# Splitting the first load of a decode kernel by partitions: 16 rows of wq first, then the other 112

## The chip, the cores and the metric

The kernel runs on one core of a Trainium2 chip. The metric is the device time of one execution in microseconds (us). Executions of this kernel fall into a fast and a slow state: the kernel before takes about 193.2 us in the one and about 196.5 us in the other, so only fast runs are compared with fast runs.

## The reference, cut to what matters

```python
g = sigmoid((x * gate_w).sum(-1))            # x: [1, 1, 512]
q = x @ wq                                   # wq: [512, 4096] bf16, 4 MB: 32 heads of 128
p = softmax(q @ k.T * 128 ** -0.5)           # k, v: [32 heads, 4096 keys, 128] bf16, 32 MB each
a = (p @ v) @ wo                             # wo: [4096, 512], 4 MB
b = relu(x @ w1 + b1) ** 2 @ w2 + b2         # w1: [512, 1376], w2: [1376, 512]
return g * a + (1 - g) * b
```

One token passes over 78.3 MB of weights and cache. Each byte is used once.

## The kernel before

The parts that the change and the argument touch, cut ("..." marks what is left out). SBUF is the memory on the core that the loads write; the large buffers of this kernel have 128 partitions. All large loads are issued by one engine (SP), so they stand in one queue (q1 of the page: 78.32 of the 78.41 MB), in the order of the code:

```python
wq_t = A_wq.rearrange("(p t) n -> p (t n)", t=4)     # 128 rows of 32 KB, contiguous in memory
wbig = sb("wbig", [128, 16384], bf16)                # one row for each SBUF partition
...
d_wq = P.dma("sp", "wq", lambda e: e.dma_start(wbig[:, :], wq_t))
...                       # q = x @ wq: 32 matmuls on TensorE; the first waits for all of d_wq
def load_k(p):            # 8 loads of [128, 16384] (32 KB a partition), two buffers
    d_k.append(P.dma("sp", f"k{p % 2}", lambda e: e.dma_start(
        Kt[:, p % 2, :], k_t[p]), prods.get((p - 2, NC - 1))))
def load_v(p):
    d_v.append(P.dma("sp", f"v{p % 2}", lambda e: e.dma_start(
        Vt[:, p % 2, :], v_t[p]), pvs.get(p - 2)))
...                       # order in the queue: wq, k0, k1, v0, k2, v1, ... k7, v6, v7
d_w1 = ...                # then w1, wo in three parts,
d_w2r = P.dma("sp", "w2r", lambda e: e.dma_start(w2_r, B_w2[128 * NJ:F, :]), k_free)
...                       # (the line above: the last 96 rows of w2, on 96 partitions) and w2 in three parts
```

The softmax here doesn't subtract the row's maximum and nothing guards it: scores larger than these inputs give would overflow.

## Time and profile before

| | the kernel before |
|---|---|
| time | 193.6 us median of 3 runs (192.99 to 193.73); 193.66 median of the 4 runs beside the change, one of them slow (196.65) |
| span of the profile shown first (slow state) | 194.5 us |
| span of a second profile, fast state, taken later as a control | 191.3 us |
| bytes loaded | 78.3 MB, 403 GB/s over the 194.5 us |

The page cuts the span into 40 equal slices. These are its lines for the DMA engines (mean busy share of the 16, in tenths) and for the rate that they moved:

```profile
DMA  6999999999999999999999999999999999999900
GB/s 216 452 431 438 438 431 445 438 438 431 428 431 431 431 431 438 431 431 431 431 421 431 431 433 426 431 431 431 431 431 421 431 431 431 395 441 404 361 33 0
```

The engines are busy from the second slice nearly to the end, and the rate stands mostly at 420 to 450 GB/s. This kernel is bound by its load stream. The same in stretches of 5 us at the start (after the length: busy us and instructions of PE, PEld, DVE, ACT and POOL, the granted clock, then, the last two columns, the DMA share and GB/s):

```profile
0.00:5.00 5.00, 0.25 (x4) 0.20 (x4) 2.44 (x7) 1.28 (x1) 3.80 (x17) 1.00 0.71 256
5.00:10.00 5.00, 0.57 (x2) 0.49 (x2) 1.35 (x2) 0.00 (x0) 0.00 (x0) 1.00 1.02 440
10.00:15.00 5.00, 1.91 (x21) 0.79 (x24) 0.00 (x0) 0.00 (x0) 0.00 (x0) 1.00 1.03 446
15.00:20.00 5.00, 1.70 (x16) 0.43 (x9) 0.48 (x3) 1.15 (x3) 0.00 (x0) 1.00 1.00 433
20.00:25.00 5.00, 0.00 (x0) 0.00 (x0) 2.29 (x2) 0.00 (x0) 0.00 (x0) 1.00 0.97 419
```

A share of 1.0 means that all sixteen engines have a packet under way, and here that goes with 420 to 446 GB/s. (A packet is counted whole where it starts, so a single stretch can be off by some per cent.)

The load of wq in the list of issues (size, then us from issue to landing), and the matmul that waits for it in the timeline (start, length, and in brackets how long the engine had been idle and what ended that):

```profile
wbig<-in_A_wq_dram SPq DMA_DIRECT2D x1, 4096.0 KB, 12.3
```

```profile
13.09 0.62 PE L178 MATMUL big<-wbig,xb 128*32 128x512 bf16 x4 [3.09 <-DMA wbig<-in_A_wq_dram]
```

The chain that ended last (start, length, what), cut to its beginning and end:

```profile
0.74 0.39 SPq L188
...
1.20 21.49 DMA Kt<-in_A_k_cache_dram
...
144.52 1.87 PE big L178 x32
...
146.41 23.37 DMA Vt<-in_A_v_cache_dram
...
191.16 0.88 PE out_ps L416 x7
...
192.06 0.48 DVE fin L446
```

In this slow-state profile the last link before the tail is the landing of the last V at 169.8 us. This is the control's chain:

```profile
0.74 0.39 SPq L188
...
1.19 21.42 DMA Kt<-in_A_k_cache_dram
...
149.77 35.75 DMA Kt<-in_B_w_dram
...
185.56 1.49 PE out_ps L416 x12
187.05 0.85 PE out_ps L442 x4
...
188.80 0.48 DVE fin L446
```

It follows the load stream to 185.5 us, where the first part of w2 lands, and 3.8 us of work follow before the result is stored (the last two parts of w2 land during this work, at 186.5 and 186.8 us).

The packets themselves are in the trace too. Every row of wq, K and V is one packet of 32 KB. I sorted the packets of this size by their end, took them in sets of sixteen (one for each engine) and give the mean end of each set, in us. For the control:

```
set            1     2     3     4     5     6     7     8     9    ...  128
before       3.85  5.06  6.27  7.48  8.69  9.91 11.12 12.33 13.54 ... 158.28
```

A set takes 1.21 us: 32 KB in 1.213 us is 27 GB/s for an engine and 432 GB/s for sixteen. Sets 1 to 8 are wq, set 9 is the first of K. Only set 1 is slow: the load is issued at 0.74 us, its packets start between 1.76 and 2.71 us and last 1.2 to 2.3 us.

### The profile page before, as it was taken

To read this page: it belongs to the slowest core of one execution; us is meant where nothing else is said; L and a number is where in the kernel's file an instruction comes from. 1 tells how busy PE (TensorE), PEld (TensorE's weight loads), DVE (VectorE), ACT (ScalarE), POOL (GpSimd) and SP (SyncE) were. 2 spreads that over 40 slices of the span, in tenths; PEclk is the share of its full clock that TensorE was granted. 3 is DMA by queue.
4 is the path that set the end of the run, shared out by engine and by line. 5 is a ranking of instruction groups with operands and counts; after the bars stand their busy time and mean duration, and the time that the engine had idled before them with its cause. 6 is when DMAs were issued, how large, how long until landed. Compare 5 with 4: busy or idle time off the path is not lost.

```text
span 194.5 us, 1358 instructions
## 1 busy us (share of the span) xinstructions
PE 114.0 (59%) x672; PEld 19.0 (10%) x424; DVE 100.0 (51%) x84; ACT 20.5 (11%) x73; POOL 3.8 (2%) x17
## 2 busy tenths in 40 slices
PE   0034086768157815981597159805880599189774
PEld 0011000001000100110001001100010011033142
DVE  5200379994098409840984098409840985001420
ACT  2002000210030013000300130003001301210010
POOL 7000000000000000000000000000000000000000
PEclk9999999999958995799669859995899579855757
DMA  6999999999999999999999999999999999999900
GB/s 216 452 431 438 438 431 445 438 438 431 428 431 431 431 431 438 431 431 431 431 421 431 431 433 426 431 431 431 431 431 421 431 431 431 395 441 404 361 33 0
DMA packets 3588, 78.41 MB, mean 403 GB/s; under 512 B 407, under 2 KB 637, under 8 KB 894
## 3 DMA queue, kind: packets, MB, share of 16 engines
q1 hardware_dynamic: 3572, 78.32, 94.3%
q8 instruction: 4, 0.07, 0.1%
q14 instruction: 2, 0.02, 0.0%
q10 hardware_dynamic: 10, 0.01, 0.0%
HBM read 78.32 MB, written 0.00 MB: 403 GB/s over the span
## 4 chain that ended last, share of the span: by engine, by line
DMA 61%; PE 20%; DVE 17%; issue 0%; ACT 0%; SPq 0%
DMA Kt<-in_A_k_cache_dram 49%; DVE prod L271 13%; PE big L180 12%; DMA Vt<-in_A_v_cache_dram 12%; DVE S L291 2%; PE qps L178 2%; PE big L178 2%; PE out_ps L416 1%; PE o_ps L324 1%; PE wo_ps L178 1%; DVE Kt L397 1%; DVE Kt L395 1%; PE out_ps L442 0%; PE misc L427 0%; ACT acc_sb L319 0%
## 5 line engine op out<-in xcount | busy, mean ns | idle before, releaser
L180 PE MATMUL big<-prod,ident 128*128 128x512 bf16 x256 | 74.9, 451 | 58.5 <-DVE prod L271 58.5
L271 DVE TENSOR_TENSOR prod<-Kt,qb 128x4096 bf16<-128x4096 bf16 x32 | 73.0, 2284 | 47.1 <-DMA Kt<-in_A_k_cache_dram 47.1
L291 DVE TENSOR_REDUCE S<-big 128x32 f32<-128x512 f32 x32 | 22.0, 686 | 8.0 <-PE big L180 8.0
L299 ACT ACTIVATE E<-S 32x128 bf16<-32x128 f32 x32 | 15.0, 470 | 99.9 <-DVE S L291 99.5
L178 PE MATMUL qps<-Vt,E 128*32 128x512 bf16 x128 | 9.3, 443 | 4.1 <-DMA Vt<-in_A_v_cache_dram 4.1
L283 PEld LDWEIGHTS <-ident 128*128 128x128 bf16 x16 | 1.6, 97 | 64.2 <-issue 64.2
L178 PE MATMUL big<-Vt,E 128*32 128x512 bf16 x128 | 7.6, 380 | 0.0
L299 ACT ACTIVATION_READ_ACCUMULATOR E<-S 32x1 f32 x32 | 7.6, 236 | 0.0
L324 PEld LDWEIGHTS o_ps<-acc_sb,pick 128*32 128x32 f32 x32 | 3.6, 124 | 38.0 <-issue 36.2
L371 DVE RECIPROCAL rden<-misc 128x1 f32<-128x1 f32 x1 | 0.2, 169 | 12.0 <-PE misc L368 12.0
L178 PEld LDWEIGHTS qps<-Vt,E 128*32 128x32 bf16 x128 | 3.5, 107 | 21.0 <-issue 19.1
L324 PE MATMUL o_ps<-acc_sb,pick 128*32 128x128 f32 x32 | 5.1, 312 | 0.7 <-ACT acc_sb L319 0.7
L178 PEld LDWEIGHTS big<-Vt,E 128*32 128x32 bf16 x128 | 3.0, 96 | 24.9 <-issue 22.2
L180 PE MATMUL big<-Kt,xb 128*128 128x512 bf16 (+1 forms) x12 | 4.7, 578 | 0.0
L251 DVE TENSOR_SCALAR gate<-gate 128x1 f32<-128x1 f32 x1 | 0.2, 153 | 8.6 <-ACT gate L250 8.6
L233 PE MATMUL misc<-xg,ones 1*128 1x1 f32 x2 | 0.6, 356 | 6.6 <-DVE xg L231 6.6
L178 PE MATMUL big<-wbig,xb 128*32 128x512 bf16 x16 | 2.6, 628 | 3.1 <-DMA wbig<-in_A_wq_dram 3.1
L319 ACT ACTIVATE acc_sb<-big 128x512 f32<-128x512 f32 x2 | 1.2, 597 | 21.2 <-PE big L178 21.2
L178 PE MATMUL wo_ps<-wbig,op_sb 128*32 128x512 bf16 x32 | 2.9, 504 | 0.5 <-DVE op_sb L393 0.5
L319 ACT ACTIVATE acc_sb<-qps 128x512 f32<-128x512 f32 x2 | 1.2, 597 | 17.6 <-PE qps L178 17.6
L393 DVE CAST op_sb<-misc 128x32 bf16<-128x32 f32 x1 | 0.3, 297 | 5.3 <-PE misc L390 5.3
L446 DVE SCALAR_TENSOR_TENSOR fin<-b_sb,gate,out_ps 128x256 bf16<-128x256 bf16 x1 | 0.5, 480 | 4.9 <-PE out_ps L416 4.9
(52 smaller groups left out, 32.7 us busy)
## 6 DMA issues: line engine op xcount, KB each, us to landing
Kt<-in_A_k_cache_dram SPq DMA_DIRECT2D x8, 4096.0 KB, 27.0
Vt<-in_A_v_cache_dram SPq DMA_DIRECT2D x8, 4096.0 KB, 32.9
wbig<-in_A_wq_dram SPq DMA_DIRECT2D x1, 4096.0 KB, 12.3
wbig<-in_A_wo_dram SPq DMA_DIRECT2D x1, 2048.0 KB, 30.7
wbig<-in_A_wo_dram SPq DMA_DIRECT2D x2, 1024.0 KB, 33.3
Kt<-in_B_w_dram SPq DMA_DIRECT2D x1, 1376.0 KB, 26.3
Kt<-in_B_w_dram SPq DMA_DIRECT2D x1, 768.0 KB, 35.7
Kt<-in_B_w_dram SPq DMA_DIRECT2D x1, 384.0 KB, 36.2
```

The lines of the kernel that those rows point to most:

```text
L178: return e.matmul(o, w, m, start=start, stop=stop, skip_group_check=True, tile_position=(0, col) if cols < 128 else None)
L180: return e.add_instruction(mybir.InstMatmult(name=nc.get_next_instruction_name(), engine=e.engine, ldweights=False, start_tensor_calc=star ...
L233: z_mm = P.add("pe", lambda e: e.matmul(z_ps, ones[0:1, :], xg[0:1, DM:DM + 1], start=True, stop=True), zr, c_one)
L271: prods[p, c] = P.add("dve", lambda e: e.tensor_tensor(prod[:, i % 2, :].rearrange("p (b d) -> p b d", d=128), Kt[:, p % 2, c * HB * 128:( ...
L283: P.add("pe", lambda e: e.ldweights(ident[:, :]), i1)
L291: sums[i] = P.add("dve", lambda e: e.tensor_reduce(S[:, p % 2, c * HB:(c + 1) * HB], red[i % 2], AX.X, ALU.add), pe_sums[i], exps.get(p - 2))
L299: exps[p] = P.add("act", lambda e, q=q, h=h: e.activation(E[q, k, :, 16 * k + h:16 * k + h + 13:4], S[q, p % 2, :].rearrange("p (g b) -> p ...
L319: copies[G] = P.add("act", lambda e: e.activation(acc_sb[:, :], acc, ACT.Copy), pvs[p], picked.get(G - 1))
L324: picked[G] = P.add("pe", lambda e, b=b: e.matmul(o_ps[32 * G:32 * G + 32, :], pick[:, b, :], acc_sb[:, 128 * b:128 * b + 128], start=(b = ...
L395: ha = P.add("dve", lambda e: e.tensor_scalar(hrelu, h_ps[0:1, :], 0.0, gate[0:1, 3:4], ALU.max, ALU.mult), hm, g3)
L397: hb = P.add("dve", lambda e: e.scalar_tensor_tensor(hsrow, h_ps[0:1, :], 0.0, hrelu, ALU.max, ALU.mult), ha)
L416: done = P.add("pe", lambda e, hh=hh: e.matmul(out_ps[64 * hh:64 * hh + 64, :], v.to_broadcast([n, 64]), w[:, 256 * hh:256 * hh + 256], st ...
```

## The change

Its intent is to have the sixteen engines start sooner: the hope was that a first load with one row (one packet) for each engine gets them going earlier, and the second load, with the other 112 rows, comes in behind it. Both add to one semaphore (a counter on which an engine can wait), and the matmul waits for both.

```diff
-        d_wq = P.dma("sp", "wq", lambda e: e.dma_start(wbig[:, :], wq_t))
+        P.dma("sp", "wq", lambda e: e.dma_start(wbig[0:16, :], wq_t[0:16]))
+        d_wq = P.dma("sp", "wq", lambda e: e.dma_start(wbig[16:128, :], wq_t[16:128]))
```

## The prediction

> **What bounds the kernel now.** The load stream. The chain that ended last is 61% DMA, the page's slices show the DMA engines 90% busy or more from 5 to 185 us, and one queue carries all large loads. The trace's packets: each 32 KB row takes 1.213 us on its engine (27 GB/s; 432 GB/s for sixteen), back to back from 3.9 us on. All K and V loads stand behind wq in that queue, so a delay of the slowest engine in wq comes back in every landing, in that of the last V (169.8 us in the chain) and, 24 us of PE tail later, in the end: factor near 1.
>
> **What the change aims at.** wq is issued at 0.74 us; its first rows start at 1.76 to 2.71 us, take 1.26 to 2.22 us in place of 1.21, and end at 3.87 us on average. One row an engine first may start all engines by about 1.8 us at full rate: my estimate from these durations is a gain of at most 0.9 us, more likely 0.3 to 0.5. The second issue costs 0.39 us of the SP queue (as the present one), hidden under the first rows; sixteen more semaphore writes of 9 ns are nothing.
>
> **What it adds.** [...] Does the trace agree that such loads hurt? The one large-queue load not on 128 partitions is the 96-row w2 remainder (1 KB rows, 180.6 to 183.0 us). Just then 8 KB packets of other loads rise from 309-319 ns to as much as 524, and 6 KB packets from about 240 to 373; elsewhere, a stall or two aside, they stay flat. [...]
>
> [...] Nothing catches up. Together +3 to +8 us, less if packets overlap well.
>
> **Prediction.** 199.5 us, range 193.0 to 203.5. Faster by over 2%: 1%; within 2%: 33%; slower by over 2%: 66%.
>
> **What the profile would show.** If right: first sixteen packets of 4 to 5 us, wq landing at 17 to 21 us instead of 13.05, K's first load at 27 to 30 instead of 22.7; some wq rows of 1.5 to 2.4 us, then 1.213 us as before, engines ending several us apart; DVE, PE and tail unchanged in length, all shifted. If the intent holds: first packets of 1.2 to 1.4 us, starts within 0.3 us, wq landing and the end 0.3 to 0.9 us earlier.
>
> **What would make it wrong.** [...] rows dealt round-robin to engines, not in blocks [...]; the skew absorbed by idle time in the queue, of which I see none.

The sum came to +3 to +8 us: its lower end stood for the 16-row load, the rest, up to 5 us, for the 112 rows. Both were estimates, from an assumption on how much a set of partitions takes in that no trace had shown. "Such loads" are loads that write fewer than the 128 partitions.

## The result, and the profile after

| | before | after |
|---|---|---|
| median | 193.66 us (4 runs, one slow) | 202.41 us (4 runs, one slow) |
| span of a fast profile | 191.3 us | 200.0 us |
| GB/s over that span | 409 | 392 |
| ratio of the fast runs | | 1.0452, 95% interval 1.0405 to 1.0499 |

A ratio is the mean time of one kernel's fast runs over that of the other's fast runs of the same rounds, so it isn't quite the ratio of the medians. 1.0452 is some 8.7 us: the changed kernel is slower by 4.5%.

The two slice lines of the page after:

```profile
DMA  7998999999999999999999999999999999999970
GB/s 105 210 315 210 406 419 419 419 426 426 459 459 416 426 426 419 426 426 452 452 433 416 426 419 428 428 433 439 452 426 419 423 433 426 433 409 426 408 285 2
```

The engines are as busy as before, but in the first four slices (5 us each) they move 105, 210, 315 and 210 GB/s. From the fifth on they move 406 to 459 GB/s until the stream ends, about as before. The stretches at the start, with the columns as before:

```profile
0.00:5.00 5.00, 0.26 (x4) 0.20 (x4) 2.45 (x7) 1.28 (x1) 3.79 (x17) 1.00 0.72 105
5.00:10.00 5.00, 0.58 (x2) 0.50 (x2) 1.35 (x2) 0.00 (x0) 0.00 (x0) 1.00 1.03 210
10.00:15.00 5.00, 0.00 (x0) 0.00 (x0) 0.00 (x0) 0.00 (x0) 0.00 (x0) 1.00 1.12 315
15.00:20.00 5.00, 0.00 (x0) 0.00 (x0) 0.00 (x0) 0.00 (x0) 0.00 (x0) 1.00 0.87 210
20.00:25.00 5.00, 2.45 (x24) 0.93 (x28) 0.00 (x0) 0.00 (x0) 0.00 (x0) 1.00 1.06 406
```

In the second stretch the share is 1.03 and the rate 210 GB/s, against 1.02 and 440 before. Packets were under way all the time, they only lasted longer. Here a busy DMA engine is no proof of moving bytes at the full rate.

The two loads of wq in the list of issues, and the matmul that waits for them:

```profile
wbig<-in_A_wq_dram SPq DMA_DIRECT2D x1, 3584.0 KB, 21.3
wbig<-in_A_wq_dram SPq DMA_DIRECT2D x1, 512.0 KB, 6.7
```

```profile
22.55 0.62 PE L178 MATMUL big<-wbig,xb 128*32 128x512 bf16 x4 [13.27 <-DMA wbig<-in_A_wq_dram]
```

The 512 KB land 6.7 us after their issue at 0.74 us, the other 3.5 MB 21.3 us after theirs at 1.21 us, at 22.5 us. Before, all 4 MB had landed at 13.0 us. The chain, cut to its beginning and end:

```profile
0.74 0.40 SPq L188
...
1.21 0.40 SPq L189
...
1.65 30.56 DMA Kt<-in_A_k_cache_dram
...
159.18 35.25 DMA Kt<-in_B_w_dram
...
194.48 1.49 PE out_ps L417 x12
195.97 0.85 PE out_ps L443 x4
...
197.50 0.48 DVE fin L447
```

It is the control's chain, link for link, with the second issue (0.40 us, hidden) and one longer wait: the first K load lands at 32.21 us in place of 22.61 us. The first part of w2 lands at 194.44 us in place of 185.52 us, and the tail after that is 3.5 us instead of 3.8. So the whole loss arises in the first 23 us and is then carried to the end. The sets of sixteen packets say the same:

```
set            1     2     3     4     5     6     7     8     9    ...  128
before       3.85  5.06  6.27  7.48  8.69  9.91 11.12 12.33 13.54 ... 158.28
after        5.50  8.35 10.62 12.41 14.23 16.22 18.45 20.55 22.33 ... 167.22
difference   1.65  3.29  4.35  4.93  5.54  6.31  7.33  8.22  8.79 ...   8.94
```

At set 9 the difference is 8.79 us, and 119 sets later it is 8.94 us. Nothing is caught up, since from then on every engine again takes 1.21 us a row.

### The profile page after: what moved, and what is told of

It reads as the page before. It is cut to its first block, busy times and chain, and to the rows that moved or that the text cites. A ratio compares the mean times of both kernels' runs of the same rounds, so it can differ in the third digit from the quotient of the medians.

```text
span 200.0 us, 1358 instructions
## 1 busy us (share of the span) xinstructions
PE 108.5 (54%) x671; PEld 17.9 (9%) x424; DVE 99.9 (50%) x84; ACT 20.6 (10%) x73; POOL 3.8 (2%) x17
## 4 chain that ended last, share of the span: by engine, by line
DMA 69%; DVE 16%; PE 10%; SPq 2%; issue 0%
DMA Kt<-in_A_k_cache_dram 52%; DMA Kt<-in_B_w_dram 18%; DVE prod L272 13%; PE big L180 8%; DVE S L292 3%; PE out_ps L417 1%; PE big L178 1%; SPq L351 1%; SPq L356 1%; PE out_ps L443 0%; DVE fin L447 0%; SPq L358 0%; SPq L188 0%; SPq L189 0%; SPq L267 0%
## 5 line engine op out<-in xcount | busy, mean ns | idle before, releaser
L180 PE MATMUL big<-prod,ident 128*128 128x512 bf16 x256 | 73.6, 446 | 59.3 <-DVE prod L272 59.3
L178 PE MATMUL qps<-Vt,E 128*32 128x512 bf16 x128 | 8.3, 402 | 4.1 <-DMA Vt<-in_A_v_cache_dram 4.1
L178 PEld LDWEIGHTS big<-Vt,E 128*32 128x32 bf16 x128 | 3.1, 96 | 25.2 <-issue 22.6
L178 PEld LDWEIGHTS qps<-Vt,E 128*32 128x32 bf16 x128 | 3.2, 98 | 21.3 <-issue 18.9
L417 PE MATMUL out_ps<-Kt,hs 128*64 128x256 bf16 (+1 forms) x22 | 2.8, 396 | 0.7 <-DMA Kt<-in_B_w_dram 0.7
L247 ACT ACTIVATE qb<-big 128x512 bf16<-128x512 f32 x1 | 0.6, 597 | 22.5 <-PE qps L178 22.5
## 6 DMA issues: line engine op xcount, KB each, us to landing
wbig<-in_A_wq_dram SPq DMA_DIRECT2D x1, 3584.0 KB, 21.3
```

Of the source, the lines that this page charges most:

```text
L178: return e.matmul(o, w, m, start=start, stop=stop, skip_group_check=True, tile_position=(0, col) if cols < 128 else None)
L180: return e.add_instruction(mybir.InstMatmult(name=nc.get_next_instruction_name(), engine=e.engine, ldweights=False, start_tensor_calc=star ...
L417: done = P.add("pe", lambda e, hh=hh: e.matmul(out_ps[64 * hh:64 * hh + 64, :], v.to_broadcast([n, 64]), w[:, 256 * hh:256 * hh + 256], st ...
```

## The experiments

My theory (theory 1 in the expectations): what counts is the set of partitions that a load writes, and loads that write fewer than all 128 are slow. Why they should be was an assumption that no run shows, with the terms worked out from it, and what they came to (such as +27 to +29 us) stands as the author's estimate. The rivals: (A) two loads or a small first load cost this by themselves; (B) the memory's side is slow, because sixteen neighbouring rows are read at once; (C) what counts is the number of rows, for example an odd number for an engine; (D), for a sign in the trace of before: small packets slow their neighbours whatever the partitions. All runs gave results that agree with the reference; two write rows of wq to wrong partitions on purpose, and the comparison didn't notice (their reported correctness says nothing about them). In the cut diffs below, `dma(a, b)` stands for `P.dma("sp", "wq", lambda e: e.dma_start(a, b))`.

### before_again: the kernel before, unchanged

> The kernel before, unchanged, as a control and for a profile in the fast state (the profile shown of before was taken in the slow state). All theories: 193 to 194 us, ratio 1.00, first sixteen rows ending at 3.9 us on average, then 1.213 us a row, wq landing at 13.0 us.

Measured: 192.95 us, ratio 0.9991 (0.9973 to 1.001), set 1 at 3.85 us, wq landed at 12.9 us. This is the control from whose fast profile I have quoted above.

### cols_first: two loads, the first of 512 KB, but cut by columns

```diff
-d_wq = dma(wbig[:, :], wq_t)
+dma(wbig[:, 0:2048], wq_t[:, 0:2048])
+d_wq = dma(wbig[:, 2048:16384], wq_t[:, 2048:16384])
```

> wq in two loads again, the first again of 512 KB, but cut by columns: 4 KB of each of the 128 partitions first, then the other 28 KB. Theory 1 ([...]only the set of partitions that a load writes matters): no loss; wq lands within 0.6 us of 13.05, the end between -0.6 and +0.4 us of before, ratio 0.997 to 1.002. Rival A (two loads behind each other, or a small first load, cost the time by themselves): wq lands at 17 us or later and the end is 4 to 9 us later, as with the change.

Measured: ratio 1.0002 (0.9983 to 1.0021); wq landed at 12.73 us, 0.18 us before the control's. The first two stretches:

```profile
0.00:5.00 5.00, 0.26 (x4) 0.20 (x4) 3.25 (x9) 1.28 (x1) 4.04 (x17) 1.00 0.78 289
5.00:10.00 5.00, 0.58 (x2) 0.49 (x2) 0.55 (x1) 0.00 (x0) 0.28 (x2) 1.00 0.88 379
```

Nothing of the 105 and 210 GB/s of the changed kernel is to be seen. Rival A is refuted: the same bytes first, the same second issue, and no loss.

### extra16: the 16-row load alone, before an unchanged load of wq

```diff
+d_dummy = dma(Vt[0:16, 1, :], wq_t[0:16])     # overwritten later by the second V load, which waits for it
 d_wq = dma(wbig[:, :], wq_t)
```

> The 16-row load alone: 16 rows of wq go to 16 partitions of a buffer that is overwritten later, then wq comes in one load of 128 partitions as before. 512 KB more are loaded than before. Bytes alone (16 rows at 1.213 us in parallel): +1.2 us at the end. Theory 1 [...] the end is +3.5 to +4.8 us; with the 3.4 to 3.8 us that these rows took in the changed kernel, +2.2 to +3.3 us. Rows of the 128-partition load afterwards 1.21 us (theory 1), or still 2 us for several rows if something other than the set of partitions slows the beginning of the program.

Measured: fast runs 196.98 and 197.56 us, ratio 1.0215 (1.0192 to 1.0237), that is +4.15 us, of which 1.21 us is the set of rows that is loaded in addition. The sets end at 5.49, 7.87, 9.08, 10.31, 11.52 us: the 16 rows and the set behind them are late, and then it is 1.21 us a set at once. Its first three stretches:

```profile
0.00:5.00 5.00, 0.29 (x4) 0.21 (x4) 2.55 (x7) 1.28 (x1) 3.79 (x17) 1.00 0.84 125
5.00:10.00 5.00, 0.58 (x2) 0.50 (x2) 1.35 (x2) 0.00 (x0) 0.00 (x0) 1.00 0.86 296
10.00:15.00 5.00, 0.00 (x0) 0.00 (x0) 0.00 (x0) 0.00 (x0) 0.00 (x0) 1.00 1.01 433
```

So the 16-row load costs 4.15 - 1.21 = 2.9 us by itself. My estimate from the four runs further below: a set on 16 neighbouring partitions takes 4.42 to 4.58 us there in place of 1.21 us, which is 3.2 to 3.4 us more, less what the slow start of the program hides (the control's first packets last 1.2 to 2.3 us as it is). The packet records alone would mislead: the 16 packets last 2.9 to 3.9 us, and the next ones, of the load on all 128 partitions, still 1.5 to 2.9 us. One set's waiting seems to be booked partly on the next.

### rows112_first: the two loads in the other order

```diff
+dma(wbig[16:128, :], wq_t[16:128])
+d_wq = dma(wbig[0:16, :], wq_t[0:16])
```

> The two loads of the change in the other order: 112 rows first, then 16. Theory 1: the 112-row load is slow by itself, 1.6 to 2.4 us a row, wq lands at 20 to 23 us and the end is +7 to +10 us, as in the changed kernel. If the 16-row load were alone to blame (its engines getting out of step, or its rows holding up what is behind it): rows of 1.2 us in the 112-row part, the end +1 to +4 us.

Measured: 202.82 us, ratio 1.0495 (1.0474 to 1.0516); wq landed at 22.6 us. The rate by slices (5 us each):

```profile
GB/s 210 301 223 177 314 432 419 426 432 419 445 439 435 432 426 426 432 419 445 432 445 429 426 426 427 427 432 426 445 432 429 426 432 432 426 400 426 411 284 0
```

The 112 rows are slow with nothing in front of them: sets 2 to 7 end 1.6 to 2.2 us apart (3.91, 6.04, 7.68, 9.44, 11.48, 13.72, 15.89 us). The 16-row load isn't alone to blame. Taking its 2.9 us from the 8.7 us of the change leaves 5.8 us for the 112 rows, or 0.83 us for each of the seven rows of an engine. This split isn't fixed, since the slow start hides part of the loss of the load that comes first (the first set ends at 3.91 us here and at 3.85 us in the control), and no run has the 112 rows alone: here, in front, their seven sets end 4.8 us late (15.89 us, against 11.12 us in the control), and the two sets behind them bring the delay to 9.0 us (22.51 against 13.54 us).

### Four runs that tell the write side from the read side

wq comes in eight loads of 16 rows. In the first run, 16 neighbouring rows of memory go to 16 neighbouring partitions; in the others the writes, the reads or both step by 8.

```diff
+for r in range(8):
+    d_wq = dma(wbig[16*r:16*r+16, :], wq_t[16*r:16*r+16, :])   # eight_w4p_rnear: neighbouring partitions, near rows
+    d_wq = dma(wbig[r:128:8, :],      wq_t[16*r:16*r+16, :])   # eight_w8p_rnear: every 8th partition, near rows (wrong rows on purpose)
+    d_wq = dma(wbig[16*r:16*r+16, :], wq_t[r:128:8, :])        # eight_w4p_rfar:  neighbouring partitions, far rows (wrong rows on purpose)
+    d_wq = dma(wbig[r:128:8, :],      wq_t[r:128:8, :])        # eight_w8p_rfar:  every 8th partition, far rows
```

(One of the four lines in each run. In the labels w4p stands for 16 neighbouring partitions and w8p for every 8th.)

> First of four that tell the write side from the read side: wq in eight loads of 16 rows, each row one packet of 32 KB, one an engine. Here 16 neighbouring rows of the memory go to 16 neighbouring partitions [...]. Theory 1 [...] the end +27 to +29 us. Rival B (the memory's side: 16 neighbouring rows read at once are slow, whatever they are written to): also slow, so this one alone doesn't tell. Number of loads alone: about 0.

> The same reads (16 neighbouring rows a load) written to partitions r, r+8, ... r+120 [...]. The result is wrong on purpose, the rows stand in other partitions. Theory 1: [...] the end +8 to +10 us. Rival B (read side): the same as the run with neighbouring partitions.

> Rows r, r+8, ... r+120 of the memory (256 KB apart) read by one load and written to 16 neighbouring partitions [...]. Wrong result on purpose. Theory 1: +27 to +29 us, as with neighbouring rows. Rival B (read side): as the run that reads far rows[...].

> Rows r, r+8, ... read and written to the same partitions r, r+8, ... ([...]the result is right). Theory 1: +8 to +10 us[...]. Rival B (read side): slow or fast with the run that reads far rows[...].

In this call the three runs of the kernel before were all at 195.1 to 196.6 us, where other calls have their slow state, so I don't use its ratios and read the stream itself (the profile of the first run is of the slow state). The time of a set is the mean over sets 2 to 8:

| writes | reads | us a set of 16 rows | fastest run |
|---|---|---|---|
| 16 neighbouring partitions | near | 4.58 | 218.79 us |
| 16 neighbouring partitions | far | 4.42 | 219.02 us |
| every 8th partition | near | 2.52 | 203.47 us |
| every 8th partition | far | 2.54 | 203.56 us |

Stretches from the middle of wq (15 to 25 us with neighbouring partitions and near rows; 20 to 25 us with far rows; 10 to 15 us with every 8th partition, near and far):

```profile
15.00:20.00 5.00, 0.00 (x0) 0.00 (x0) 0.00 (x0) 0.00 (x0) 0.00 (x0) 1.00 1.04 118
20.00:25.00 5.00, 0.00 (x0) 0.00 (x0) 0.00 (x0) 0.00 (x0) 0.00 (x0) 1.00 0.98 111
```

```profile
20.00:25.00 5.00, 0.00 (x0) 0.00 (x0) 0.00 (x0) 0.00 (x0) 0.00 (x0) 1.00 0.89 105
```

```profile
10.00:15.00 5.00, 0.00 (x0) 0.00 (x0) 0.00 (x0) 0.00 (x0) 0.00 (x0) 1.00 0.98 210
```

```profile
10.00:15.00 5.00, 0.00 (x0) 0.00 (x0) 0.00 (x0) 0.00 (x0) 0.00 (x0) 1.00 1.02 216
```

The partitions decide, and the reads hardly matter: rival B is refuted. The runs on neighbouring partitions lost a little less than expected (about 25.7 us on the 193.2 us, expected 27 to 29) and those on every 8th partition a little more (10.3 us, expected 8 to 10). As rates, a set of 512 KB came in at 114 to 119 GB/s on 16 neighbouring partitions and at 206 to 208 GB/s on every 8th, against 432 GB/s in the control's load of 128. Why the partitions decide, these runs don't tell.

### halves: two loads of 64 partitions

```diff
+dma(wbig[0:64, :], wq_t[0:64])
+d_wq = dma(wbig[64:128, :], wq_t[64:128])
```

> wq as two loads of 64 neighbouring partitions, 4 rows an engine, nothing like 16 or 112. Theory 1: [...] 2.43 to 2.55 us a row (8 rows), wq in 19.4 to 20.4 us instead of 9.7, the end +9 to +10.5 us. Rival C (only loads with a row count that is odd for the engine, such as 7 rows, or with single rows, are slow; 64 rows is 4 an engine): the end within 1 us of before.

Measured: 203.44 and 203.67 us, ratio 1.0534 (1.0509 to 1.056), 2.54 us a set. Its second stretch:

```profile
5.00:10.00 5.00, 0.58 (x2) 0.50 (x2) 1.35 (x2) 0.00 (x0) 0.00 (x0) 1.00 1.00 204
```

Two loads of 64 rows are slower than the change with its 16 and 112, and as slow as eight loads of every 8th partition. Rival C is refuted. Nor does the number of loads matter: two loads cost 2.54 us a set here, eight cost 2.52 to 2.54.

### stride7: how the 112 rows are dealt

```diff
 dma(wbig[0:16, :], wq_t[0:16])
-d_wq = dma(wbig[16:128, :], wq_t[16:128])
+for r in range(7):
+    d_wq = dma(wbig[16+r:128:7, :], wq_t[16+r:128:7, :])
```

> How the 112 rows are dealt to the engines. The 16-row load as in the change, then seven loads of 16 rows with a step of 7 partitions (16+r, 23+r, ... ): what a 112-row load does if each engine gets a block of 7 neighbouring rows. If the change's second load is dealt in blocks: the same rows of 1.8 to 2.3 us, wq landing at 20 to 23 us, the end +8 to +10 us, within 1 us of the changed kernel. If it is dealt otherwise: a different time a row; [...] (Round-robin dealing is already refuted by the 4.4 to 4.6 us a row that loads of 16 neighbouring partitions took.)

Measured: one fast run of 201.68 us (the profile fell in the slow state; the first 25 us are read from it, where the stream alone counts). The sets beside those of the changed kernel:

```
set            1     2     3     4     5     6     7     8     9
after        5.50  8.35 10.62 12.41 14.23 16.22 18.45 20.55 22.33
stride7      5.58  8.40 10.69 12.50 14.28 16.28 18.53 20.62 22.37
```

```profile
5.00:10.00 5.00, 0.58 (x2) 0.49 (x2) 1.35 (x2) 0.00 (x0) 0.00 (x0) 1.00 1.04 211
10.00:15.00 5.00, 0.00 (x0) 0.00 (x0) 0.00 (x0) 0.00 (x0) 0.00 (x0) 1.00 1.12 315
15.00:20.00 5.00, 0.00 (x0) 0.00 (x0) 0.00 (x0) 0.00 (x0) 0.00 (x0) 1.00 0.87 210
```

Seven loads whose row r goes to partitions 16+r, 23+r, 30+r ... behave as the one load of 112 rows does, set by set within 0.1 us. So that load is dealt in blocks of seven neighbouring rows, or in a way that can't be told from it. These loads answer one more rival, for which no run was made: that what counts is how close together the partitions of a set lie. A step of 8 took 2.5 us a set and a step of 7 takes 1.8 to 2.3 us (sets 3 to 8), although its partitions lie closer. What fell here is my hand model of what follows (an estimate whose basis no run shows): it slowed only some of the engines and let the others run at 1.21 us, so that the engines would end rows apart. In both kernels all engines are slowed nearly alike (in the changed one the packets of sets 3 to 8 last 1.63 to 2.40 us); the last set of wq's rows in the changed kernel ends within 1.2 us (20.18 to 21.37 us). (With the 112 rows in front, in rows112_first, they drift a little: its seventh set ends within 2.3 us.)

### cols_small: 1 KB of each partition first

```diff
+dma(wbig[:, 0:512], wq_t[:, 0:512])
+d_wq = dma(wbig[:, 512:16384], wq_t[:, 512:16384])
```

> The intent of the change[...] with a smaller first load: 1 KB of each partition first (128 KB), then 31 KB. If the first rows are slow because one large load takes long to be laid out for the engines: the engines are at full rate earlier, wq lands 0.3 to 0.6 us before 12.9 us, the end 0.997 to 0.999. If the slow start is a ramp of the whole system that lasts until about 2.5 us whatever is loaded (as the 4 KB packets of the run with columns suggest, 156 to 904 ns until then, 159 ns after): wq lands within 0.3 us of 12.9 us, ratio 0.998 to 1.002.

Measured: ratio 1.0002 (0.9978 to 1.0025), wq landed at 13.30 us, 0.4 us later than the control's, so neither expectation of the landing holds fully; the gain of 0.3 to 0.6 us isn't there. With cols_first, where single 4 KB packets can be seen, packets last 156 to 904 ns until about 2.7 us and 159 ns after. The slow start is thus no matter of the size of the first load. What causes it, no run tells.

### w2r_128: the one load of the kernel before that isn't on 128 partitions

```diff
-w2_r = part(DM)[0:FT, :]                       # FT = 96
+w2_r = part(DM)
-d_w2r = dma(w2_r, B_w2[128 * NJ:F, :])
+d_w2r = dma(w2_r, B_w2[F - 128:F, :])          # 32 rows twice; their factors in hs are set to 0 (that edit is left out here)
```

> The kernel before with its one load that isn't on 128 partitions mended: the 96-row remainder of w2 becomes the last 128 rows of w2 (32 of them loaded twice; their factors are set to 0, so the result is right). It tests the sign that the prediction read in the trace of before. Theory 1: while these rows come in, the 8 KB packets beside them stay at 309 to 320 ns (up to 524 before) and the 6 KB packets at about 240 (mean 278, up to 380 before); the last w2 rows land 0.2 to 0.5 us earlier and the end, which waits for them in the fast state, comes 0 to 0.5 us earlier, ratio 0.997 to 1.000. Rival D (small packets as such slow their neighbours, whatever the partitions): the packets rise as before, and 32 KB more are loaded, ratio 1.000 to 1.002.

Measured: the 8 KB packets beside these rows last at most 322 ns, the 6 KB packets 242 ns on average and at most 262 (in the control the 8 KB packets beside these rows went up to 487 ns and the 6 KB packets to 380, 278 on average). This profile is of the slow state, so I set it beside the slow profile of before: the stretches 180:181 and 181:182 us of before and then of this run:

```profile
180.00:181.00 1.00, 1.00 (x5) 0.04 (x1) 0.00 (x0) 0.00 (x0) 0.00 (x0) 0.50 1.05 414
181.00:182.00 1.00, 1.00 (x4) 0.11 (x1) 0.00 (x0) 0.00 (x0) 0.00 (x0) 0.50 1.00 326
```

```profile
180.00:181.00 1.00, 1.00 (x5) 0.05 (x1) 0.00 (x0) 0.00 (x0) 0.00 (x0) 0.50 1.01 410
181.00:182.00 1.00, 1.00 (x4) 0.10 (x1) 0.00 (x0) 0.00 (x0) 0.00 (x0) 0.50 1.06 420
```

In the second stretch 326 GB/s becomes 420 though more is loaded (the control, in the fast state, has 388 and 339): rival D is refuted, and the sign that the prediction had read in the trace of before was one of the 96 partitions: with these rows on 128 it is gone. The first part of w2 lands at 185.26 us, in the slow profile of before at 185.44 us and in the control at 185.52 us. On the time this is at the limit of what can be told: six fast runs at 192.74 to 193.56 us, ratio 0.9953 with an interval from 0.9892 to 1.0015. The interval is that wide because two runs of the kernel before at 195.4 and 195.7 us were counted as fast. It is the only changed version tried with a median below that of the kernel before (192.81 to 193.37 us), and it isn't shown to be faster.

## Why the prediction was right

**The time.** 199.5 us was predicted with a range to 203.5, 202.41 us was measured; "slower by over 2%" had 66%. That the set of partitions written costs the time was right (why it does was assumed, and no run shows it), but the size was partly luck: the prediction's own sum, +3 to +8 us on 193.7 us, ends at 201.7 us, below what was measured. Only the margin that the range has beyond its sum took it in.

**"Factor near 1": right, and shown.** 8.79 us at the ninth set of packets, 8.94 us at the 128th, 8.7 us between the spans. The route was read from a slow-state profile, with "24 us of PE tail" after the last V; in the fast state the chain runs on through the w2 load, and the work after that is 3.5 to 3.8 us. The conclusion is the same, because both follow the stream.

**The lower end of the sum, +3 us, for the 16-row load: about right.** 2.9 us, from the 16-row load alone (extra16). What this term was worked out from is not shown by any run, so the agreement doesn't speak for it. That the partitions written decide was argued in the prediction and is now shown by the four runs that separate writes from reads: 4.4 to 4.6 us a set on 16 neighbouring partitions, 2.5 on every 8th, whatever is read.

**The rest of the sum, up to 5 us, for the 112 rows: too small.** It came to 5.8 us behind the 16 rows (a difference, 8.7 - 2.9) and to at least 4.8 us in front of them, and on all engines. The dealing in blocks of seven agrees with stride7; the step that failed is the hand model, which slowed only some of the engines. This is why wq landed at 22.5 us (17 to 21 were named) and K's first load at 32.2 (27 to 30), and why the sum came to 8.7 us and not to "3 to 8".

**"Engines ending several us apart": wrong.** They end within 1.2 us. The sets of the changed kernel behind the 16-row load take 2.85, 2.27, 1.79, 1.82, 1.99, 2.23 and 2.10 us (the first still holds waiting for the 16 rows): the third and the fourth of the seven are the fastest, as they are in rows112_first (1.64 and 1.76 us). No packet of these rows lasts under 1.6 us, so none of them keeps to the 1.21 us of the load of 128 partitions. Why all engines are slowed, and why these two sets less than the others, stays open.

**"First sixteen packets of 4 to 5 us": not as predicted.** They last 3.3 to 3.8 us and the next set 2.6 to 3.2; the total of this load (2.9 us more, in extra16) was about right and its booking on packets wrong.

**The gain that was hoped for.** The prediction allowed 0.3 to 0.5 us if the intent held. With columns, where nothing stands against it, the larger first load brought wq forward by 0.18 us and the smaller one brought nothing, and neither changed the time. Two profiles of the unchanged kernel differ by 0.14 us in this landing (13.05 and 12.91 us), so the 0.18 us is no shown gain.

## What to carry to other kernels

Cut a load by columns, not by partitions, and let each piece reach all 128 partitions: here the two loads by columns cost nothing (ratio 1.0002) and two loads of 64 partitions took 2.54 us a set of wq in place of 1.21. Read a DMA engine's busy share together with GB/s, for here the share stayed at 1.0 while the rate was halved (1.02 at 440 GB/s before, 1.03 at 210 after). In a kernel whose stream never pauses, as this one, what is lost in its first microseconds is still missing at the end (8.79 us at set 9, 8.94 us at set 128).
